# q of eight heads at a time by 64-row TensorE tiles, with VectorE's order set by deadlines, in an attention, mixer and MLP kernel

## The chip, the cores and the metric

One Trainium2 chip, one core. The metric is the device time of one execution in microseconds (us); lower is better. A kernel is run several times. With one core, a run counts as slow when it lies over 1.5% above the fastest of its kernel. A ratio is the mean time of one kernel's fast runs over the mean of the other's fast runs of the same rounds (for the experiments without the profiled run), so it isn't quite the ratio of the medians that are quoted beside it.

## The reference

```python
xn = layernorm(x)                                  # x [1, 2048, 576]
q  = xn @ wq                                       # 32 heads of 128; wq [576, 4096]
p  = softmax(q @ k.T * 128**-0.5)                  # k, v: the last 512 positions of the cache, 16 kv heads
s  = (p @ v).reshape(1, 2048, 4096) @ wo           # wo [4096, 576]
h  = gelu(layernorm(xn) @ w1)                      # mixer, w1 [576, 576]
hs = concat(the four quarters of h, shifted by 1, -1, 2, -2 rows) @ w2
x1 = xn + hs
g  = silu(x1 + gelu(layernorm(x1) @ w3) @ w4)      # MLP, w3 [576, 4608], w4 [4608, 576]
out = x + s * g
```

D is 576 = 4.5 x 128, so a contraction over D by 128-row matmuls has a last chunk that is half zeros. And the 2048 rows are done in four query blocks of 512; a block has 32 heads, called heads 0 to 31, 32 to 63 and so on.

## The kernel before

The parts that the change and the argument touch (cuts are marked `# ...`). q is made one head ahead, by five 128-row matmuls; scores of four key chunks, exps on ScalarE, values of two row tiles at a time, their evacuation on VectorE, and a DMA transpose of the head's output on SyncE's queue:

```python
def stage_q(u):
    # ...
    for kc in range(NDC):                                       # NDC = 5
        nc.tensor.matmul(psq[:, :], lhsT=w[:, kc, ...], rhs=xT_b[qb % 2][:, kc, :], ...)
    # copy to qT: VectorE in the first block, ScalarE in the others
def stage_s(u, kc):
    nc.tensor.matmul(sc[:, :], lhsT=kT[:, g, ...], rhs=qT_t[u][:, :], ...)
    nc.scalar.activation(out=pT[:, :], in_=sc[:, :], func=ACT.Exp, scale=SCALE)
def stage_v(u, t0):                                             # two row tiles of four matmuls each
    # ...
    with tc.high_priority(offset=HP):
        nc.vector.reciprocal(out=ri, in_=po[:, :, Dh])
        nc.vector.tensor_tensor(out=o[:, t0:t0 + 2, :], in0=po[:, :, 0:Dh], in1=ri..., op=ALU.mult)
def stage_t(u):
    nc.sync.dma_start(out=oT[:], in_=o[:]..., transpose=True)
```

In the first block, fetches of wq, wo, V, K and the mixer's w1 go on beside the heads, issued by GpSimd. A tiny copy of a head's first exp tile (`late`) holds GpSimd back until that head is reached:

```python
at(2, lambda: late(pT_t[2][0][0:1, 0:1], load_w1))
for i in range(8):
    at(4 + 3 * i, lambda i=i: late(pT_t[4 + 3 * i][0][0:1, 0:1], lambda: load_wo(i)))   # nc.gpsimd.dma_start
for j in range(2, NB * 8):
    at(4 * (j - 1) - 1, lambda j=j: load_wq(j))                                          # wq of 4 heads
```

Of the kernel before, what the change touches and what calls it, by code (L numbers as in the profile page):

```python
# [31 lines left out]
def kernel(  # L32
# [43 lines left out]
    PAD = 2  # L76
    VW = Dh + 2
    HP = 1500
# [20 lines left out]
    def rsqrt_newton(pool, var, n):  # L99
        v = pool.tile([P, n], FP32, name="nr_v")  # L100
        nc.vector.tensor_scalar(out=v[:], in0=var, scalar1=1.0, scalar2=LN_EPS, op0=ALU.mult, op1=ALU.add)
        y = pool.tile([P, n], FP32, name="nr_y")
        nc.vector.tensor_scalar(out=y[:].bitcast(I32), in0=v[:].bitcast(I32), scalar1=-0.5, scalar2=RSQRT_MAGIC,
                                op0=ALU.mult, op1=ALU.add)
        for _ in range(3):
            t = pool.tile([P, n], FP32, name="nr_t")
            nc.vector.scalar_tensor_tensor(out=t[:], in0=y[:], scalar=-0.5, in1=y[:], op0=ALU.mult, op1=ALU.mult)
            nc.vector.tensor_tensor(out=t[:], in0=t[:], in1=v[:], op=ALU.mult)
            y2 = pool.tile([P, n], FP32, name="nr_y")
            nc.vector.scalar_tensor_tensor(out=y2[:], in0=t[:], scalar=1.5, in1=y[:], op0=ALU.add, op1=ALU.mult)  # L110
            y = y2
        return y

    def rsqrt_table(pool, var, n):
        y = pool.tile([P, n], FP32, name="nr_y")
        nc.scalar.activation(out=y[:], in_=var, func=ACT.Sqrt, bias=eps_t[:])
        nc.vector.reciprocal(out=y[:], in_=y[:])
        e = pool.tile([P, 1], FP32, name="nr_e")
        nc.scalar.activation(out=e[:], in_=y[:, 0:1], func=ACT.Exp, scale=0.0)
        return y  # L120

    def layernorm_steps(pool, dsts, srcs, rsqrt=rsqrt_newton, twice=False):
        n = len(srcs)
        hw = D // 2
        st_ = {}

        def stats(i):
            if i == 0:
                st_["mv"] = pool.tile([P, n, 2], FP32, name="ln_mv")
            st = pool.tile([P, 2, 6], FP32, name="ln_st")  # L130
            for j in range(2):
                tc.keep_in_program_order(
                    nc.vector.bn_stats(out=st[:, j, :], in_=srcs[i][:, j * hw:(j + 1) * hw]))
            nc.vector.bn_aggr(out=st_["mv"][:, i, :], in_=st[:])

        def inv():
            st_["r"] = rsqrt(pool, st_["mv"][:, :, 1], n)

        def apply(i):
            parts = [(dsts[i], srcs[i])]  # L140
            if twice:
                parts = [(dsts[i][:, 0:D], srcs[i]), (dsts[i][:, D:DP], srcs[i][:, NF * P:D])]
            for dst, src in parts:
                nc.vector.tensor_scalar(out=dst, in0=src, scalar1=st_["mv"][:, i, 0:1],
                                        scalar2=st_["r"][:, i:i + 1], op0=ALU.subtract, op1=ALU.mult)

        return ([lambda i=i: stats(i) for i in range(n)] + [inv] + [lambda i=i: apply(i) for i in range(n)])

    def layernorm_small_steps(pool, dsts, srcs):

        n = len(srcs)
        hw = D // 2
        s = {}
        mv = pool.tile([P, n, 2], FP32, name="ln_mv")

        def stats(i, j):
            if j == 0:
                s["st"] = pool.tile([P, 2, 6], FP32, name="ln_st")
            nc.vector.bn_stats(out=s["st"][:, j, :], in_=srcs[i][:, j * hw:(j + 1) * hw])
            if j == 1:  # L160
                nc.vector.bn_aggr(out=mv[:, i, :], in_=s["st"][:])

        def begin():
            s["v"] = pool.tile([P, n], FP32, name="nr_v")
            nc.vector.tensor_scalar(out=s["v"][:], in0=mv[:, :, 1], scalar1=1.0, scalar2=LN_EPS, op0=ALU.mult,
                                    op1=ALU.add)
            s["y"] = pool.tile([P, n], FP32, name="nr_y")
            nc.vector.tensor_scalar(out=s["y"][:].bitcast(I32), in0=s["v"][:].bitcast(I32), scalar1=-0.5,
                                    scalar2=RSQRT_MAGIC, op0=ALU.mult, op1=ALU.add)

        def newton():
            y = s["y"]
            t = pool.tile([P, n], FP32, name="nr_t")
            nc.vector.scalar_tensor_tensor(out=t[:], in0=y[:], scalar=-0.5, in1=y[:], op0=ALU.mult, op1=ALU.mult)
            nc.vector.tensor_tensor(out=t[:], in0=t[:], in1=s["v"][:], op=ALU.mult)
            s["y"] = pool.tile([P, n], FP32, name="nr_y")
            nc.vector.scalar_tensor_tensor(out=s["y"][:], in0=t[:], scalar=1.5, in1=y[:], op0=ALU.add, op1=ALU.mult)

        def apply(i):
            for dst, src in [(dsts[i][:, D:DP], srcs[i][:, NF * P:D]), (dsts[i][:, 0:D], srcs[i])]:  # L180
                nc.vector.tensor_scalar(out=dst, in0=src, scalar1=mv[:, i, 0:1], scalar2=s["y"][:, i:i + 1],
                                        op0=ALU.subtract, op1=ALU.mult)

        return ([lambda i=i, j=j: stats(i, j) for i in range(n) for j in range(2)] + [begin, newton, newton, newton] +
                [lambda i=i: apply(i) for i in range(n)])

# [7 lines left out]
    xn_b = [keep.tile([P, TB, DP], BF16, name=f"xn_b{i}") for i in range(2)]  # L194
    xnn_b = keep.tile([P, TB, DP], BF16, name="xnn_b")
# [4 lines left out]
    xm_b = [xnn_b, xn_b[0]]  # L200
# [6 lines left out]
    def ln3_steps(b):  # L207
        xm = xm_b[b % 2]
        dsts, srcs = [xm[:, tt, :] for tt in range(TB)], [x1_t[b][:, tt, :] for tt in range(TB)]
        return layernorm_small_steps(small, dsts, srcs) if b else layernorm_steps(small, dsts, srcs, twice=True)  # L210

    def ln3_transpose(b):
        for tt in range(TB):
            nc.sync.dma_start(out=xT_b[b % 2][:, :, tt * P:(tt + 1) * P], in_=xm_b[b % 2][:, tt, :], transpose=True)

    with ExitStack() as actx:
# [17 lines left out]
        xraw = pool("xraw", 4)  # L234
        qT_pool = pool("qT_pool", 3)
        pT_pool = pool("pT_pool", 10)
        o_pool = pool("o_pool", 8)
        hb_pool = pool("hb_pool", 2)
        hs_pool = pool("hs_pool", 1)
        g1_pool = pool("g1_pool", 1)  # L240
# [11 lines left out]
        def load_x(b, eng):  # L252
            x_t[b] = []
            for tt in range(TB):
                xt = xraw.tile([P, D], BF16, name="xt")
                t = b * TB + tt
                eng.dma_start(out=xt[:], in_=x2[t * P:(t + 1) * P, :])
                x_t[b].append(xt)

        def load_wq(j, eng=None):  # L260
# [5 lines left out]
            eng.dma_start(out=w[0:DR, NF, :], in_=A_wq[NF * P:D, c0:c0 + 4 * Dh])  # L266
# [17 lines left out]
        def prep_k(g):  # L284
# [3 lines left out]
            def tr(kc):  # L288
# [4 lines left out]
                if kc == KCH - 1:  # L293
# [3 lines left out]
                    with tc.high_priority(offset=HP):  # L297
                        nc.vector.tensor_copy(out=kT[:, g, :], in_=st["ps"][:, :])
# [3 lines left out]
        def late(ap, fn):  # L302
            g = nc.gpsimd.tensor_copy(out=gate[:, :], in_=ap)
            with tc.issue_after(g.ins):
                fn()

        x_t[0] = []
        for tt in range(TB):
            xt = xraw.tile([P, D], BF16, name="xt")
# [809 lines left out]
```

## Time and profile before

| | |
|---|---|
| median of the first three runs | 846.1 us (843.39 to 848.49) |
| span of the profiled run | 842.4 us |
| TensorE, ScalarE, VectorE busy | 98, 55, 51% |
| attention and mixer, MLP and tail | 11.6 to 552.2, 552.2 to 842.4 us |

The prediction shows the lines that it rests on. One view it didn't take is the busy time by stage, with the first query block by itself: the first row is the first block (heads 0 to 31), the second the other three with the output projection, the third the MLP. A row gives the stretch and its length, the busy time of each engine with its instructions, the granted clock, the mean busy share of the DMA engines (the time that their packets took, over the time of 16 engines; it can exceed 1), and what they moved in GB/s.

```profile
11.60:115.30 103.70, 101.91 (x864) 63.93 (x881) 82.11 (x263) 77.59 (x138) 30.69 (x52) 1.00 0.90 185
115.30:552.20 436.90, 433.22 (x3603) 256.36 (x3663) 202.65 (x698) 278.70 (x512) 39.85 (x65) 1.00 0.47 102
552.20:842.40 290.20, 283.04 (x3348) 157.70 (x3349) 137.05 (x370) 100.63 (x170) 0.00 (x0) 1.00 0.22 60
```

TensorE is full in every stage. But the DMA engines are 90% busy in the first block, against 47 and 22% later. The page's own row of 40 slices says the same in its first five digits, if one looks at it: 6, 9, 9, 7, 8.

### The profile page before, as it was taken

How to read it: one execution, taken by the hardware profiler on the slowest of the kernel's cores; microseconds unless marked ns; L12 is line 12 of the kernel's file. 1: busy time of each engine (PE TensorE's matmuls, PEld its weight loads, DVE VectorE, ACT ScalarE, POOL GpSimd, SP SyncE). 2: the span in 40 equal slices, each digit the busy share in tenths (PEclk: the TensorE clock that was granted, in tenths of full speed). 3: DMA queues.
4: the chain of work that ended last, by engine and by line, in shares of the span. 5: the costliest groups of instructions: out<-in, count | busy, mean ns of one | idle time of the engine just before them, and what ended most of it. 6: DMA issues, size and time to landing. Idle time of an engine off the chain costs nothing.

```text
span 842.4 us, 19365 instructions
## 1 busy us (share of the span) xinstructions
PE 827.0 (98%) x7896; PEld 486.5 (58%) x7980; DVE 427.8 (51%) x1351; ACT 460.9 (55%) x825; POOL 76.5 (9%) x134
## 2 busy tenths in 40 slices
PE   8999999999999999999999999999999999999996
PEld 6665655665665566565566555455555555555555
DVE  5789941258751156772144884034246636555334
ACT  4776773498793388885369874033233333334610
POOL 3532213010010111010001100000000000000000
PEclk9999999999999999999999999999999999999999
DMA  6997862173372174363148336993001321230101
GB/s 173 228 248 163 147 137 65 56 137 90 87 135 46 41 131 97 89 121 79 29 87 160 67 85 106 282 340 83 2 2 44 64 69 44 46 87 16 44 15 46
DMA packets 139983, 83.94 MB, mean 100 GB/s; under 512 B 106944, under 2 KB 133248, under 8 KB 139888
## 3 DMA queue, kind: packets, MB, share of 16 engines
q1 hardware_dynamic: 130048, 53.01, 31.2%
q0 software_dynamic: 8448, 28.15, 11.9%
q8 instruction: 64, 1.05, 0.5%
q10 hardware_dynamic: 1392, 1.48, 0.5%
q14 instruction: 31, 0.25, 0.1%
HBM read 49.17 MB, written 9.44 MB: 70 GB/s over the span
## 4 chain that ended last, share of the span: by engine, by line

## 5 line engine op out<-in xcount | busy, mean ns | idle before, releaser
L404 ACT ACTIVATE pT<-sc 128x512 bf16<-128x512 f32 x512 | 290.3, 596 | 101.5 <-PE sc L402 89.5
L402 PE MATMUL sc<-qT,kT 128*128 128x512 bf16 x492 | 174.6, 378 | 1.3 <-DVE qT L392 0.6
L419 PEld LDWEIGHTS <-pT 128*128 128x128 bf16 x2048 | 139.6, 98 | 50.7 <-ACT pT L404 0.4
L419 PE MATMUL po<-v_sb,pT 128*128 128x129 bf16 x2048 | 161.4, 220 | 1.3 <-ACT pT L404 0.3
L387 PE MATMUL psq<-xT_b,wq_b 128*128 128x512 bf16 x604 | 152.4, 379 | 2.2 <-DVE xT_b L369 0.3
L423 DVE RECIPROCAL ri_b<-po 128x2 f32<-128x2 f32 x256 | 43.1, 168 | 188.8 <-PE po L419 184.5
L772 PE MATMUL ph<-xT_b,w_s 64*128 64x512 bf16 x976 | 127.1, 376 | 0.2 <-DVE hx L788 0.2
L809 PE MATMUL pm<-w_s,h 64*128 64x512 bf16 x864 | 122.3, 377 | 0.0
L443 PE MATMUL pswo<-wo_sb,oT 128*128 128x512 bf16 x497 | 114.2, 379 | 0.7
L424 DVE TENSOR_TENSOR o<-po,ri_b 128x256 bf16<-128x256 f32 x256 | 107.9, 422 | 6.5 <-DVE ri_b L423 0.3
L790 ACT ACTIVATE h<-ph 128x512 bf16<-128x512 f32 x67 | 39.4, 597 | 130.4 <-PE ph L772 130.4
L387 PEld LDWEIGHTS <-wq_b 128*128 128x128 bf16 x640 | 62.3, 98 | 74.3 <-issue 2.3
L809 PEld LDWEIGHTS <-h 64*128 64x128 bf16 x1728 | 70.7, 94 | 55.6 <-issue 0.4
L443 PEld LDWEIGHTS <-oT 128*128 128x128 bf16 x1024 | 65.0, 98 | 55.1 <-DMA oT<-o 0.2
L809 PE MATMUL pr<-w_s,h 64*128 64x64 bf16 x864 | 90.1, 189 | 0.2 <-ACT h L790 0.2
L772 PEld LDWEIGHTS <-w_s 64*128 64x128 bf16 x1152 | 57.2, 94 | 48.6 <-issue 0.5
L788 DVE COPY hx<-ph 128x512 f32<-128x512 f32 x55 | 38.0, 692 | 69.6 <-PE ph L772 69.6
L394 ACT ACTIVATE qT<-psq 128x512 bf16<-128x512 f32 x96 | 57.4, 598 | 27.8 <-PE psq L387 26.8
L402 PEld LDWEIGHTS <-kT 128*128 128x128 bf16 x512 | 47.4, 97 | 28.3 <-DVE qT L392 1.1
L264 POOL DMA_DIRECT2D wq_b<-in_A_wq_dram x30 | 23.3, 778 | 312.3 <-PE psq L387 293.5
L790 ACT ACTIVATE h<-hx 128x512 bf16<-128x512 f32 x55 | 34.6, 630 | 8.3 <-DVE hx L788 6.4
L762 DVE TENSOR_SCALAR fence<-ph,ph 1x1 f32<-1x1 f32 x61 | 12.8, 210 | 49.9 <-PE ph L772 49.4
(124 smaller groups left out, 645.4 us busy)
## 6 DMA issues: line engine op xcount, KB each, us to landing
wq_b<-in_A_wq_dram POOLq DMA_DIRECT2D x30, 512.0 KB, 5.2
w_s<-in_B_w_dram SPq DMA_DIRECT2D x9, 576.0 KB, 7.1
wo_sb<-in_A_wo_dram POOLq DMA_DIRECT2D x8, 576.0 KB, 5.0
w_s<-in_B_w_dram SPq DMA_DIRECT2D x9, 512.0 KB, 7.9
x_dram<-x SPq DMA_DIRECT2D x4, 576.0 KB, 3.5
x<-x_dram SPq DMA_DIRECT2D x4, 576.0 KB, 5.0
s_b<-s_dram SPq DMA_DIRECT2D x4, 576.0 KB, 5.6
x_b<-in_A_x_dram SPq DMA_DIRECT2D x4, 576.0 KB, 6.3
```

The lines of the kernel that those rows point to most:

```text
L387: nc.tensor.matmul(psq[:, :], lhsT=w[:, kc, hh * Dh:(hh + 1) * Dh], rhs=xT_b[qb % 2][:, kc, :], start=(kc == 0), stop=(kc == NDC - 1))
L394: nc.scalar.activation(out=qT[:, :], in_=psq[:, :], func=ACT.Copy)
L402: nc.tensor.matmul(sc[:, :], lhsT=kT[:, g, kc * P:(kc + 1) * P], rhs=qT_t[u][:, :], start=True, stop=True)
L404: nc.scalar.activation(out=pT[:, :], in_=sc[:, :], func=ACT.Exp, scale=SCALE)
L419: nc.tensor.matmul(po[:, j, :], lhsT=pTs[kc][:, tt * P:(tt + 1) * P], rhs=v_sb[:, g, kc, 0:Dh + 1], start=(kc == 0), stop=(kc == KCH - 1))
L423: nc.vector.reciprocal(out=ri, in_=po[:, :, Dh])
L424: nc.vector.tensor_tensor(out=o[:, t0:t0 + 2, :], in0=po[:, :, 0:Dh], in1=ri.unsqueeze(2).to_broadcast([P, 2, Dh]), op=ALU.mult)
L443: nc.tensor.matmul(ps, lhsT=oT_t[qb * Hq + h][:, tt, :], rhs=wo_sb[:, h, lo:hi], start=(h == 0), stop=(h == Hq - 1))
L772: nc.tensor.matmul(ps[i][:, :], lhsT=lhsT, rhs=xT[half, kc, :], start=first, stop=last, skip_group_check=True)
L788: nc.vector.tensor_copy(out=src[:, :], in_=ps[i][:, :])
L790: nc.scalar.activation(out=h3[:, :], in_=src[:, :], func=ACT.Gelu_apprx_tanh)
L809: nc.tensor.matmul(out, lhsT=h3_t[b, fc][half, tt * P:(tt + 1) * P], rhs=w4_s[fc // WS][half, fc % WS, lo:hi], start=key not in started, s ...
```

## The change

Its intent: two heads share the half chunk of D (64-row tiles that run in pairs), which takes 64 of 640 q slots off TensorE. To make that possible, q comes in groups of four heads in the first block and of eight later, gelu is written in place and buffers are shared so that eight q tiles fit, values come one row tile at a time and half a head later, and VectorE's and ScalarE's order is no longer loose but fixed, with layernorm and gelu steps let in by deadlines and a budget of time. The core of the diff, cut:

```diff
-            eng.dma_start(out=w[0:DR, NF, :], in_=A_wq[NF * P:D, c0:c0 + 4 * Dh])
+            for half in (LO, HI):
+                eng.dma_start(out=w[half, NF, :], in_=A_wq[NF * P:D, c0:c0 + 4 * Dh])
-        qT_pool = pool("qT_pool", 3)
+        qT_pool = pool("qT_pool", 8)
-        o_pool = pool("o_pool", 8)
+        o_pool = pool("o_pool", 9)
+        def stage_qs(u0, n):
+            # pairs of heads; banks X, Y, Z, X
+                    q_half(xT, u, ps, [(kc, ((0, LO), (1, HI))) for kc in range(NDC)], True)
+                    nc.vector.tensor_scalar(out=f[:, :], in0=ps[0][0:1, 0:1], scalar1=ps[1][0:1, 0:1], ...)  # fence
+                    unit(0.7)                       # up to 0.7 us of layernorm or gelu steps on VectorE
+                # ...
+                    q_half(xT, u, ps, [(kc, ((1, LO), (0, HI))) for kc in range(NF)], False)
+                    nc.scalar.activation(out=qT_t[u][:, :], in_=ps[0][:, :], func=ACT.Copy)
+                    nc.vector.tensor_copy(out=qT_t[u + 1][:, :], in_=ps[1][:, :])
-        at(2, lambda: late(pT_t[2][0][0:1, 0:1], load_w1))
-        at(10, gather_w1)
+        at(13, lambda: late(pT_t[13][0][0:1, 0:1], load_w1))
+        at(20, gather_w1)
-            at(4 + 3 * i, ... load_wo(i)))
+            at(9 + 3 * i, ... load_wo(i)))
-            at(4 * (j - 1) - 1, lambda j=j: load_wq(j))
+            at(4 * (j - 2) + 1 if j < 10 else 8 * (j // 2 - 1) + 1 + j % 2, lambda j=j: load_wq(j))
-        with tc.manual_schedule(engines={SP, POOL, PE}):
+        with tc.manual_schedule(engines={SP, POOL, PE, DVE, ACTE}):
+                if u % (4 if u < Hq else 8) == 0 and 0 < u < U:
+                    stage_qs(u, 4 if u < Hq else 8)
+                    v, tt = (u - 2, 2 + i) if i < 2 else (u - 1, i - 2)
```

## The prediction

> **What bounds the kernel now.** I read the page's busy table first, then TensorE's waits, then one head in the timeline, then the groups by line.
>
> ```profile
> PE 827.0 (98%) x7896; PEld 486.5 (58%) x7980; DVE 427.8 (51%) x1351; ACT 460.9 (55%) x825; POOL 76.5 (9%) x134
> ...
> PE warm L672 <- POOL ident masks.py:199: 1.6, 1, 1.6
> PE ps_k L291 <- DMA x<-in_A_k_cache_dram: 0.9, 1, 0.9
> PE sc L402 <- DVE qT L392: 0.6, 1, 0.6
> PE psq L387 <- DVE xT_b L369: 0.3, 1, 0.3
> PE sc L402 <- ACT pT L404: 0.3, 1, 0.3
> ```
>
> TensorE has work for 98% of the span, and its list of waits is short: the largest five (shown) sum to 3.7 us, nearly all in the first 16 us. So no wait can be shortened for profit, and time must come out of TensorE's own instruction slots. Busy time alone doesn't prove that the slots are dense, because a 512-column matmul is shown as 0.378 us and overlaps its successor. The timeline of one head in the second query block shows the spacing:
>
> ```profile
> 303.46 0.38 PE L402 MATMUL sc<-qT,kT 128*128 128x512 bf16 x1
> ...
> 303.67 0.63 PE L419 MATMUL po<-v_sb,pT 128*128 128x129 bf16 x8
> ...
> 304.14 0.38 PE L402 MATMUL sc<-qT,kT 128*128 128x512 bf16 x1
> ...
> 305.26 1.24 PE L387 MATMUL psq<-xT_b,wq_b 128*128 128x512 bf16 x5
> ...
> 306.34 0.38 PE L402 MATMUL sc<-qT,kT 128*128 128x512 bf16 x1
> ...
> 307.77 1.58 ACT L404 ACTIVATE pT<-sc 128x512 bf16<-128x512 f32 x3
> ```
>
> A head repeats every 306.34 - 303.46 = 2.88 us. Five q matmuls take 1.24, so one slot is (1.24 - 0.38)/4 = 0.215 us. Eight value matmuls fill 303.67 to 304.14, so one is 0.059. The head's slots are 5 x 0.216 for q + 4 x 0.216 for scores + 16 x 0.059 for values = 1.08 + 0.86 + 0.94 = 2.88 us: the measured period, with no gap. ScalarE's three exps in 1.58 us, one being 0.596 in the groups, give (1.58 - 0.596)/2 = 0.49 us apiece when they are queued.
>
> Summed over attention and mixer, with counts from the loops: q 640 x 0.216 = 138, scores 512 x 0.216 = 111, values 2048 x 0.059 = 120, output projection 512 x 0.216 + 512 x 0.029 = 125, mixer 180 x 0.216 + 80 x 0.029 = 41, K transposes 4, together 539 us. The first q is at 11.6 and the MLP starts at 552.3 (its row is below): 541 us. The MLP and its tail, to 842.4, are not changed.
>
> ```profile
> 551.32 1.01 PE L443 MATMUL pswr<-wo_sb,oT 128*128 128x64 bf16 x29
> 552.26 1.04 PE L772 MATMUL ph<-xT_b,w_s 64*128 64x512 bf16 x8
> 553.13 0.38 PE L772 MATMUL ph<-xT_b,w3r_s 64*128 64x512 bf16 x2
> ...
> 799.34 1.04 PE L772 MATMUL ph<-xT_b,w_s 64*128 64x512 bf16 x8
> 800.32 0.39 PE L972 MATMUL pm<-w_s,h 128*128 128x512 bf16 x1
> ```
>
> These rows are also the only two places where the kernel changes between 128-row and 64-row matmuls.
>
> **What the Trainium skill says.** "TensorE: Matmul & The Clock Gate", Part 3 on packing small matmuls, says that matmuls in distinct row groups run concurrently. The trace agrees: eight 64-row matmuls take 553.13 - 552.26 = 0.87 us, so a pair takes one slot of 0.217. "TensorEngine Tiling (Array Packing)", Key Properties, says that a change of tiling mode drains TensorE. The trace agrees and sizes it: the 29 narrow matmuls are (1.01 - 0.19)/28 = 0.029 apart, the last starts at 552.14, and the next, of 64 rows, only at 552.26, that is 0.12 against 0.03; on the way back four pairs from 799.34 should end at 800.20 and the next starts at 800.32. About 0.1 us each way. The same page, Gotcha 1, says that different row tiles must not access one PSUM bank at the same time; the kernel before already puts a tiny VectorE fence (210 ns) between the halves that swap banks in the MLP. Lastly, the first page says that ScalarE and VectorE are strict FIFO; so a wrongly placed VectorE instruction delays those behind it. No wait of the trace tests that as the order is now loose.
>
> **The change part by part.**
> (1) q by 64-row tiles. D is 576 = 4.5 chunks of 128 rows, and the fifth q matmul of each head is half zeros. Two heads now share the work: 9 half chunks x 2 heads = 18 half matmuls = 9 pair slots instead of 10. Over 128 heads: 64 slots x 0.216 = 13.8 us saved, all on the bound.
> (2) Mode switches. Eight groups of 4 heads in the first block and four groups of 8 in each of three others are 20 groups, 40 switches x 0.1 = +4.0 us. Some will hide in waits of (4).
> (3) Fences. 64 x 0.21 = 13 us more of VectorE. While one fence runs, TensorE does the other pair: the fence of the second pair must come within the first pair's second half, 4 slots = 0.86 us, against about 0.2 latency + 0.21 + at most 0.7 of an instruction ahead. It should be hidden.
> (4) ScalarE's pace. Before, q (1.08 us) stood between the scores of each head, giving ScalarE 2.88 us for four exps and a copy, 4 x 0.49 + 0.6 = 2.6. Now q comes in a lump of 36 slots = 7.8 us per 8 heads, in which ScalarE has only up to three leftover scores and four copies. Between lumps, a head without other TensorE work is 0.86 + 0.94 = 1.80 us for TensorE and 1.97 for ScalarE: 0.17 us of wait. Of the last three blocks' 96 heads about 60 have no filler by the new slots (the output projection sits in five heads of a block, the mixer in about ten). A group's start adds 0.3 (ScalarE's last q copy), and a run-ahead of three score banks takes away about 0.5. I count 1.3 + 1.9 + 1.3 us for these blocks. In the first block, q also takes two of the three score banks, hence waits for two exps: ScalarE's cycle per 4 heads is about 12.2 against 11.8 us, +0.4 in eight groups = 3.2. Sum of this part about +7.5 at most.
> (5) One bank for the output projection. Its evacuation (0.6 + 0.2 of latency) used to lie behind a q lump; now only a score and four values (0.45 us) stand in between, unless mixer atoms follow. Five such places x 0.4 = +2.
> (6) VectorE's order. VectorE gains 13 us of fences, 32 x 0.69 = 22 us of q copies (ScalarE loses as many) and 5 of zero padding: 428 to 468, 56% of the span. It isn't the bound, but a pair of value groups now comes every 0.9 us with a 0.6 us evacuation and two banks. A wide instruction in between can hold TensorE by 0.1 or 0.2. I give it +2.
> (7) In-place gelu, in-place layernorm, shared buffers: the same instructions; they pay with SBUF for eight q tiles. Nine instead of eight attention outputs give transposes slack: issuing one takes 1.2 us on the queue, a head at least 1.8, so no gain of its own.
> (8) Start: waits of 0.6 + 0.3 + 0.3 at the first heads go, -1; the last head's values come half a head later, +0.5.
> Parts (4) to (6) hold the same engine and overlap: while TensorE waits for a bank, ScalarE catches up. Of their 11.5 I keep 7. Sum: -13.8 + 4.0 + 7 - 0.5 = -3.3, that is 846.1 - 3.3 = 842.8; I say 842.
>
> **Rivals.** A: the waits are tuned away, the gain is slots less switches: 846.1 - 13.8 + 4.0 - 1 = 835. For it: the slots of the mixer are placed unevenly, as if by trial, and a deadline order looks made for this. Against: 0.17 us in each unfilled head isn't removable by order. B: ScalarE becomes the bound wherever there is no filler and the terms add fully, or the strict order on VectorE and ScalarE (a tanh queued ahead of exps while its input is late) stalls TensorE; 846.1 - 13.8 + 4 + 11.5 + 4 = 852. For it: ScalarE has 290 us of exps in some 510 us and is idle for about half of the lumps. Against: four copies fall into the lumps. C: the half matmuls don't pair (each needs its own weight load, 64 pairs more of them): then q costs more than before and the time rises by some 10 us. Against: the MLP's 64-row matmuls pair at 0.217.
>
> **Range and chances.** The floor is 835 less one or two, the upper rival 852. So 842, with 833 to 851 for 8 in 10. Faster by over 2% would be below 829, more than the whole saving of 13.8: 2%. Slower by over 2% is above 863, which takes stalls of 27 us: 4%. Within 2%: 94%.
>
> **What would show it.** q rows as 64-row matmuls, 18 per two heads at 0.108 us each; the first 64-row matmul of a lump about 0.1 late. TensorE's wait list, nearly empty now, should name the exps (score bank, and values waiting for exps) with 5 to 8 us in the heads without filler, and the output projection waiting for its own evacuation with about 2. The MLP should start near 548 instead of 552 and take the same 290 us. Wrong: if TensorE's waits on VectorE (fences, value evacuation) exceed those on ScalarE, part (6) was under-sized; if waits are under 3 us in all, rival A holds; if the MLP's length changes, I have missed something.

## The result, and the profile after

| | before | after |
|---|---|---|
| median | 844.91 us (4 runs) | 875.82 us (4 runs: 869.92, 871.14, 880.5, and 883.55, slow) |
| ratio of fast runs | | 1.0336, 95% interval 1.024 to 1.0432: slower |
| profiled run | 842.4 us span | 868.1 us span |
| first block | 103.7 us | 111.5 us |
| later blocks | 436.9 us | 454.6 us |
| MLP and tail | 290.2 us | 290.2 us |

The predicted 842 and its range up to 851 are missed. The same view by stage, for the changed kernel:

```profile
11.80:123.30 111.50, 100.14 (x967) 62.22 (x977) 71.87 (x242) 74.51 (x148) 35.23 (x60) 0.95 0.99 165
123.30:577.90 454.60, 440.62 (x4043) 258.69 (x4085) 258.80 (x824) 249.81 (x470) 50.29 (x86) 1.00 0.47 105
577.90:868.10 290.20, 282.63 (x3345) 161.88 (x3346) 137.71 (x374) 100.38 (x170) 1.09 (x1) 0.99 0.22 60
```

So the loss has two places: 7.8 us in the first block, where TensorE's busy time shrank while its clock fell to 0.95 and the DMA share rose to 0.99 with fewer GB/s (165 for 185), and 17.7 in the later blocks, where VectorE now has 258.8 us for 202.7. The MLP is untouched. TensorE's waits (us in total, times, longest), nearly empty before, name engines for both:

```profile
PE psq L444 <- DMA wq_b<-in_A_wq_dram: 7.3, 3, 5.2
PE po L469 <- DVE o L476: 6.5, 9, 1.4
PE psx L615 <- DVE x L626: 3.0, 5, 0.9
PE po L469 <- issue: 1.9, 12, 0.2
PE psq L444 <- DMA xT_b<-xn_b: 1.7, 1, 1.7
...
PE pswo L497 <- ACT x L511: 0.9, 4, 0.2
PE sc L452 <- ACT pT L454: 0.7, 1, 0.7
```

**The first block.** Its groups of four heads (from a group's first q matmul to the next group's) take 12.4, 12.1, 12.1, 12.1, 12.1, 14.4, 20.8 and 15.5 us: at first the pace that was predicted (12.2), and then a stall of some 12 us (11.5 against the first block of the run without a stall, h2_spq below). By stretches of the span, same columns as above:

```profile
20.00:55.00 35.00, 34.84 (x357) 22.64 (x358) 27.66 (x95) 25.87 (x53) 11.45 (x20) 1.00 0.77 154
55.00:75.00 20.00, 19.95 (x210) 13.18 (x210) 15.94 (x59) 15.20 (x31) 11.70 (x20) 1.00 1.10 205
75.00:95.00 20.00, 11.78 (x117) 7.07 (x116) 8.79 (x31) 9.14 (x18) 3.51 (x6) 0.85 1.06 113
```

In the third stretch the DMA engines are as busy as in the second and move little more than half as much, and TensorE works 11.78 of 20 us. The timeline shows the chain: SyncE's queue takes 37 us to issue six output transposes (the kernel before took 1.2 to 2.4 each); VectorE waits 7.42 us for an output buffer to be read out; TensorE waits 5.25 us for weights of the next q group.

```profile
59.69 37.33 SPq L486 DMA_TRANSPOSE oT<-o  x6
...
93.22 0.42 DVE L476 TENSOR_TENSOR o<-po,ri_b 128x256 bf16<-128x256 f32 x1 [7.42 <-DMA oT<-o]
...
94.46 5.57 PE L444 MATMUL psq<-xT_b,wq_b 64*128 64x512 bf16 x27 [5.25 <-DMA wq_b<-in_A_wq_dram]
```

The page's table of DMA issues gives KB and the median from issue to landing; the kernel before had 5.0 in the first of these two rows and 3.1 in the second:

```profile
wo_sb<-in_A_wo_dram POOLq DMA_DIRECT2D x8, 576.0 KB, 10.6
...
oT<-o SPq DMA_TRANSPOSE x128, 2.7
```

The row of `oT<-o` is a trap. Its median over the whole span even fell; but of the 32 transposes issued between 20 and 115 us, 13 landed after more than 9 us and the latest after 29.8. Before, none of 38 was above 9.0.

Not all of the 11.5 us is waiting. The granted clock was 0.50 from 89.1 to 99.3 us, so when the weights had come at 94.5 TensorE worked at this half clock for 4.8 us more, which I estimate from these figures at 2.4 us lost:

```profile
90.00:95.00 5.00, 0.54 (x4) 0.27 (x6) 0.75 (x2) 0.00 (x0) 0.00 (x0) 0.50 0.78 133
95.00:100.00 5.00, 5.00 (x28) 1.66 (x25) 1.26 (x4) 0.60 (x1) 0.00 (x0) 0.57 1.20 186
```

Other traces have such stretches, of 3.4 us or more, in the later blocks too. They are named below where they bear on a comparison.

**The later blocks.** The list of waits sums to some 12 us there, less than the loss. The rest is gaps too short for it: a 512-column matmul is drawn as 0.378 us, so a successor that is 0.27 us late isn't seen as late. The timeline of heads without filling work shows ScalarE with twelve exps end to end, and the scores at its pace:

```profile
363.35 6.04 ACT L454 ACTIVATE pT<-sc 128x512 bf16<-128x512 f32 x12
...
365.03 0.38 PE L452 MATMUL sc<-qT,kT 128*128 128x512 bf16 x1
...
366.01 0.38 PE L452 MATMUL sc<-qT,kT 128*128 128x512 bf16 x1
...
366.99 0.38 PE L452 MATMUL sc<-qT,kT 128*128 128x512 bf16 x1
```

Two scores per 0.98 us, where the slots of two scores and two groups of four values are 0.90. And where the mixer's second product has one bank, TensorE waits for VectorE to add it to xn and free the bank:

```profile
506.55 0.68 DVE L626 TENSOR_TENSOR x<-psx,xn_b 128x512 bf16<-128x512 f32 x1
507.28 1.02 PE L615 MATMUL psx<-w_sb,hb 128*128 128x512 bf16 x4 [0.93 <-DVE x L626]
```

I therefore took, for every matmul, the time to the next one's start less its slot, and added it up by the kinds of the two. In the later blocks (of the one-queue run below, which has them as the changed kernel does): scores followed by values 6.1 us (the bank that VectorE must free), values followed by scores 5.5 (ScalarE), values followed by the mixer's product 5.1, values followed by the output projection 3.1 (its one bank), going into 64-row mode 0.85 over nine and out about 1.3 over twelve, other kinds about 1. That is some 23. The same count gives 3.9 us in the kernel before.

### The profile page after: what moved, and what is told of

Its sections match the earlier page's. It is cut to its first block, busy times and chain, and to the rows that moved or that the text cites.

```text
span 868.1 us, 20505 instructions
## 1 busy us (share of the span) xinstructions
PE 831.8 (96%) x8436; PEld 490.2 (56%) x8492; DVE 475.4 (55%) x1463; ACT 428.6 (49%) x793; POOL 91.3 (11%) x161
## 4 chain that ended last, share of the span: by engine, by line
## 5 line engine op out<-in xcount | busy, mean ns | idle before, releaser
L454 ACT ACTIVATE pT<-sc 128x512 bf16<-128x512 f32 x512 | 266.8, 668 | 91.4 <-PE sc L452 89.8
L469 PE MATMUL po<-v_sb,pT 128*128 128x129 bf16 x2048 | 202.5, 220 | 9.0 <-DVE o L476 6.5
L469 PEld LDWEIGHTS <-pT 128*128 128x128 bf16 x2048 | 157.3, 97 | 82.4 <-DVE o L476 11.2
L452 PE MATMUL sc<-qT,kT 128*128 128x512 bf16 x489 | 184.6, 378 | 1.3 <-ACT pT L454 0.7
L444 PE MATMUL psq<-xT_b,wq_b 64*128 64x512 bf16 x1152 | 132.9, 381 | 9.9 <-DMA wq_b<-in_A_wq_dram 7.3
L476 DVE TENSOR_TENSOR o<-po,ri_b 128x256 bf16<-128x256 f32 x256 | 108.6, 424 | 17.7 <-DMA oT<-o 8.7
L868 PEld LDWEIGHTS <-h 64*128 64x128 bf16 x1728 | 73.5, 94 | 52.9 <-issue 0.3
L444 PEld LDWEIGHTS <-wq_b 64*128 64x128 bf16 x1152 | 58.7, 95 | 77.1 <-issue 8.4
L436 ACT ACTIVATE qT<-psq 128x512 bf16<-128x512 f32 x64 | 38.2, 597 | 96.7 <-PE psq L444 94.2
L452 PEld LDWEIGHTS <-kT 128*128 128x128 bf16 x512 | 49.9, 98 | 21.3 <-issue 8.8
L437 DVE CAST qT<-psq 128x512 bf16<-128x512 f32 x64 | 44.1, 690 | 18.4 <-PE psq L444 18.2
```

The source lines that it names most:

```text
L436: nc.scalar.activation(out=qT_t[u][:, :], in_=ps[0][:, :], func=ACT.Copy)
L437: nc.vector.tensor_copy(out=qT_t[u + 1][:, :], in_=ps[1][:, :])
L444: nc.tensor.matmul(ps[k][:, :], lhsT=w[half, kc, hh * Dh:(hh + 1) * Dh], rhs=xT[half, kc, :], start=(first and kc == 0), stop=(not first a ...
L452: nc.tensor.matmul(sc[:, :], lhsT=kT[:, g, kc * P:(kc + 1) * P], rhs=qT_t[u][:, :], start=True, stop=True)
L469: nc.tensor.matmul(po[:, j, :], lhsT=pTs[kc][:, tt * P:(tt + 1) * P], rhs=v_sb[:, g, kc, 0:Dh + 1], start=(kc == 0), stop=(kc == KCH - 1))
L868: nc.tensor.matmul(out, lhsT=h3_t[b, fc][half, tt * P:(tt + 1) * P], rhs=w4_s[fc // WS][half, fc % WS, lo:hi], start=key not in started, s ...
```

## The experiments

Two numbers from the packets of a trace serve in all of them, for 20 to 115 or 125 us: how late output and layernorm transposes land, and for how long both kinds of packets are in flight at a time (in steps of 0.25 us; more than two of each), with what each kind moved meanwhile. The table holds them, in the order of this section.

| run | us, median | transposes: latest landing, number over 9 us | both in flight, us | fetched + transposed then, KB per us |
|---|---|---|---|---|
| before | 844.91 | 9.0, 0 of 38 | 15.5 | 102 + 79 |
| after | 875.82 | 29.8, 13 of 32 | 38.5 | 117 + 42 |
| e1_loads | 889.87 | 27.6, 17 of 24 | 55.5 | 119 + 31 |
| b_late | 853.83 (fast runs 844.6, profiled, and 848.33) | 10.8, 3 of 38 | 17.2 | 126 + 72 |
| e2_q128 | 886.78 | 28.6, 14 of 25 | 65.0 | 117 + 29 |
| e3_b2banks | 885.22 | 26.5, 17 of 23 | 40.2 | 110 + 44 |
| f2_wo_first | 873.03, and 892.91, slow (profiled) | 26.2, 19 of 20 | 74.0 | 91 + 28 |
| f3_o4 | 877.72 and 880.44 | 25.2, 7 of 32 | 34.2 | 101 + 42 |
| g1_paced | 869.42 | 27.0, 10 of 31 | 42.0 | 123 + 42 |
| g2_block0 | 874.07 | 28.0, 15 of 30 | 56.2 | 114 + 40 |
| g4_relief2 | 871.65 | 12.9, 4 of 38 (the profiled run, 860.89) | 30.8 | 92 + 55 |
| h1_quarter_wo | 859.48 | 23.6, 12 of 33 | 42.2 | 90 + 42 |
| h4_before_more | 852.29 | 12.7, 8 of 33 | 22.2 | 138 + 72 |
| h2_spq | 857.46 | 7.4, 0 of 38 | 14.0 | 119 + 105 |
| i1_actq | 877.06 | 7.7, 0 of 33 | 15.2 | 106 + 86 |

With one kind alone in flight, the kernel before moves 289 KB per us of fetches, or 142 of transposes.

### Is the stall a matter of when the fetches come?

My first theory was that the later places of wo and w1 crowd the fetches. The first run puts them back, the second gives the kernel before the later places.

```diff
 e1_loads (from the changed kernel)
-        at(13, ... load_w1))
+        at(2, ... load_w1))
-            at(9 + 3 * i, ... load_wo(i)))
+            at(4 + 3 * i, ... load_wo(i)))
 b_late (from the kernel before)
-        at(2, ... load_w1))
+        at(10, ... load_w1))
-            at(4 + 3 * i, ... load_wo(i)))
+            at(9 + 3 * i, ... load_wo(i)))
```

> The changed kernel with one edit: the output projection's weights and w1 are fetched five and eleven heads earlier in the first block, as in the kernel before. Theory 1 (crowded loads): in the changed kernel about 15 us of the 25 us lost before the MLP come from 72 to 123 us, where oT transposes took up to 30 us to land, value evacuations waited 9 us for them and q 7 us for wq; the cause is that the fetches start late and pile up. Then this kernel lies near 855 us, transposes land within about 10 us and TensorE no longer waits for wq. Rival (the two half-row fetches of wq's last chunk, or the denser transposes, overload the queues whatever the timing): 868 to 876 and the same long landings.

> The mirror of it: the kernel before, with the output projection's weights fetched five heads later and w1 eight heads later. Theory 1: landing times of its transposes rise well over 10 us around 55 to 95 us and it loses some 5 to 15 us against 844. Rival (timing of the fetches doesn't matter): within 1 us of 844.

Measured: e1_loads 889.87 us, ratio 1.0533, so worse; the stall came earlier, with 22.9 us of VectorE's waits for output buffers and 21.9 us of TensorE's on VectorE's evacuation (16.2 of them in the first block). b_late 853.83, its profiled run 844.6 without a stall; two of its runs, 859.33 and 859.73, count as slow, and the ratio, 1.0106 (1.0021 to 1.0191), has them in it. Its fast runs, 844.6 and 848.33, lie among the kernel before's of the same rounds (843.39 to 850.76), so no loss is shown. The theory falls: the old places don't cure the changed kernel, and the new ones aren't shown to harm the old kernel.

### Is it the 64-row q, the half-row fetch, or VectorE?

Both from e1_loads: q by 128-row matmuls in the same groups, without fence and without the second fetch of the half chunk; and a second bank for the mixer's second product.

```diff
 e2_q128
-                    q_half(xT, u, ps, [(kc, ((0, LO), (1, HI))) ...      # and the fence, and the second half
+                    q_full(xT, u, ps)          # for k in 0, 1: five matmuls lhsT=w[:, kc, ...], rhs=xT[:, kc, :]
 e3_b2banks
-                    st["ps"] = ps_wo.tile([P, M0], FP32, name="psx1", tag="wo")
+                    psp, tag = (ps_pq, "pq") if tt % 2 else (ps_wo, "wo")
+                    st["ps"] = psp.tile([P, M0], FP32, name="psx1", tag=tag)
```

> The first experiment, with q again by five 128-row matmuls per head, in the same groups of 8 heads, without fences and without the second half-row fetch. Theory (as predicted: 64 slots of 0.216 saved, 40 mode switches of 0.1 paid): slower than the first experiment by 13.8 - 4.0 = about 10 us. Rival (64-row matmuls with fences bring less, or their waits eat it): slower by under 4 us.

> The first experiment, with the mixer's second product alternating between two accumulator banks instead of one. Theory 2: its TensorE waits for VectorE's evacuation, about 4.5 us in the changed kernel, go, and the kernel is 3 to 4 us faster than the first experiment. Rival (VectorE's strict order holds TensorE anyway and the wait moves to the value evacuation): within 1.5 us of it.

Measured: e2_q128 886.78 us, three of four runs slow, the profiled one too; but the eleven group periods of the later blocks can be compared where the granted clock is alike. At full clock they take 402.6 us in e2_q128 and 397.4 in the changed kernel, whose later blocks are those of e1_loads. e1_loads has 399.0 and e3_b2banks (885.22 us) 395.3, each with 3.4 us at half clock in its last group. So 64-row tiles save 5.2 us there, switches included, where the prediction's terms (1) and (2) give 7.3 for eleven groups; and a second bank for the mixer gives 3.7. Both still stall in the first block, so the stall needs neither the half-row fetch nor that one bank.

### A spoiled run, and two on fetches and buffers

f1_block0 gave q of the first block per head again, but I left the wq fetches where groups of four need them.

```diff
 f1_block0
+        def stage_q(u): ...            # five 128-row matmuls per head, in the first block
 f2_wo_first
-            at(9 + 3 * i, ... load_wo(i)))
+            at(i // 4, ... load_wo(i)))
 f3_o4
-        o_pool = pool("o_pool", 9)
+        o_pool = pool("o_pool", 4)
```

> The changed kernel with its first block of 32 heads as before: q per head, one head ahead, by five 128-row matmuls; blocks two to four keep groups of 8 heads by 64-row tiles. Fetching earlier made the jam worse (first experiment), so theory 1 fell. Theory 1b (lumps of q make the heads between them follow each other every 2.0 instead of 2.9 us, so transposes and fetches of the first block, near the limit of the DMA engines already, arrive in bursts and the queue never drains): the jam is gone, landings below 12 us, the first block takes about 104 us instead of 111 to 127, and the time is 852 to 858. Rival (the jam comes from something else of the change: in-place layernorm, shared buffers, nine output buffers, the two half fetches, the looser fetch order): the jam stays and the time is 868 or more.

> The changed kernel with all eight fetches of the output projection's weights in the first two heads (16 to 30 us), when the DMA engines are nearly idle. Theory 1b: 4.7 MB less of fetches in the crowded stretch; the jam is gone or much shorter, 853 to 862. Rival (it isn't the amount of fetches, but deep queues of transposes beside any fetch): about as before, 868 or more.

> The changed kernel with four instead of nine buffers for attention outputs, so that no more than four transposes can wait in the queue. Theory 1b (DMA is over-subscribed, buffers only hide it): TensorE waits earlier and longer, 870 to 890. Rival (many queued transposes themselves cause the slow landings): landings stay under 12 us and the time falls below 865.

f1_block0 took 929.25 us, and its waits say why:

```profile
PE psq L444 <- DMA wq_b<-in_A_wq_dram: 60.6, 8, 16.2
```

A fetch was placed ahead of its buffer's last reader in program order, so heads waited for, and used, the next group's weights; that it passed the comparison shows only that the comparison is coarse there. It tells nothing on the stall; g2_block0 below is the mended form. f2_wo_first (873.03, and 892.91, slow) keeps the stall with all of wo fetched in the first two heads. f3_o4 (877.72 and 880.44) keeps it with four output buffers, so a deep queue of transposes isn't what starts it.

### Does another order of the last layernorm help?

From the changed kernel, with two banks for the mixer, and the MLP's first layernorm moved behind the last head:

```diff
-        at(3 * Hq + 18, lambda: push(U - 3, ln_chain(lambda: ln3_steps(0), ...)))
+        at(U, lambda: push(U, ln_chain(lambda: ln3_steps(0), ...)))
```

> The changed kernel with the mixer's second product in two banks (worth 3.7 us in blocks two to four of an earlier pair of traces) and the MLP's first layernorm moved from the last heads to the final output projection, where VectorE idles. Theory 2 (VectorE's fixed order puts filler ahead of the value evacuation, where the heads leave it only 0.25 us in 0.9): from the start of the fifth-last block boundary, that is from the first q of the second block to the MLP, 454.6 us falls by 7 to 8 to about 447. Rival (the waits come back elsewhere): it falls by less than 4.5. The total stays noisy because of the first block.

880.04 us, ratio 1.0416. From the second block's first q to the MLP it took 458.5 us, where about 447 was expected. The last group's period fell from 32.0 to 27.5 us (31.8 with the two banks alone, in e3_b2banks), as VectorE had less between the values; but from there to the MLP it took 64.8 us for 57.3, with 6.8 us at half clock and a new wait, because the layernorm's transposes now stood on SyncE's queue ahead of the MLP's weights:

```profile
PE ph L832 <- DMA w_s<-in_B_w_dram: 4.3, 1, 4.3
```

The wait moved and was not removed.

### Bursts, the grouping of q, and relief for VectorE

The second theory on the stall: some 3 MB asked for within 8 us start a backlog. g1_paced spreads the fetches, about one per head; g2_block0 is the mended f1_block0, with q per head and the kernel before's places for every fetch of the first block; the other two add relief for VectorE in the later blocks to each.

```diff
 g1_paced
-            at(9 + 3 * i, ... load_wo(i)))                 # w1 from head 13 to 11; V from heads 0, 4, ... 20
+            uw = [2, 6, 10, 14, 16, 19, 22, 26][i]         # to heads 0, 3, 8, 15, 18, 23, each gated
 g2_block0
+            stage_q(u + 1)                                 # per head in the first block
+            at(4 * (j - 1) - 1 if j < 10 else ..., load_wq(j))    # w1 at 2, wo at 4 + 3 i, as before the change
 g3_relief = g1_paced, g4_relief2 = g2_block0, each with
-                    unit(0.7)
+                    unit(1.2)
-                    nc.vector.tensor_copy(out=qT_t[u + 1][:, :], in_=ps[1][:, :])
+                    nc.scalar.activation(out=qT_t[u + 1][:, :], ...)    # but for a group's last pair
+                    # and the two banks of e3_b2banks
```

> The changed kernel with nothing but its fetches in the first block spread out, about one per head (w1 at head 11, the eight parts of wo at heads 2, 6, 10, 14, 16, 19, 22 and 26, the V heads each where no other fetch is), so that no eight microseconds ask for more than about 2 MB. Theory 'burst' (the first block's stall is a backlog that starts when about 3 MB are asked for in a row): the stall is gone or down to a few microseconds, output transposes land within 12 us all through the first block, the first 32 heads take about 112 us and the kernel 853 to 860 us. Rival (the first block's demand as a whole, with groups of four heads that run at an even pace, is more than the queues deliver, however it is spread): a stall of 10 us or more stays and the kernel takes 868 us or more.

> A corrected form of the first-block run that was spoiled: the changed kernel with q of the first 32 heads made per head by five 128-row matmuls, as before the change, and with the kernel before's heads for every fetch of that block (wq, wo, w1); later blocks as in the changed kernel. If the stall belongs to q by groups of four together with the fetches it pulls forward: the first block runs as in the kernel before (about 104 us from head 0 to head 31, no wait for wq over 1 us) and the kernel takes 852 to 860 us, of which the later blocks' loss of about 18 us against the kernel before is the remainder. Rival (the nine output buffers, the in-place x, the order of VectorE or another part stalls the first block by itself): 868 us or more with waits for output buffers still there.

> The paced kernel with three reliefs for VectorE in the later blocks: the mixer's second product takes its banks in turn from two pools, all but the last two copies of a group's q are made by ScalarE, and filler steps of a group come in lumps of at most 1.2 us rather than 0.7. Theory (VectorE's queue in the later blocks, not TensorE's slots, costs some 11 us there: about 7 before the value matmuls and 4.5 before the mixer's bank): from the first q of the second block to the MLP's first matmul it takes 446 to 449 us in place of 454.6. Rival (ScalarE, whose exponentials are the pace there, takes over what VectorE gives up): 452 us or more, with the wait of the scores' banks longer by what the other waits lose.

> The corrected first-block form with the same three reliefs: if both losses are what I take them for, they add up: first block as in the kernel before, later blocks 6 to 8 us shorter than in the changed kernel, 844 to 852 us in all. Rival (they are one loss in two places): no faster than the better of the two runs it is made of.

Measured: g1_paced 869.42 us (864.62 to 873.37), ratio 1.0284: the stall stays, transposes land as late as 27 us. The burst theory falls. g2_block0 874.07, ratio 1.0398: so the grouping of q with its earlier fetches isn't the cause either. g3_relief 879.97, ratio 1.0405, and g4_relief2 871.65 (its profiled run 860.89, with a small stall), ratio 1.0332. From the second block's first q to the MLP it took 455.0, 456.2, 455.1 and 455.4 us in the four runs: the reliefs together gave nothing. The second bank's gain was given back in the second block's last group, 31.9 us for 28.3, where the waits for value banks rose from 1.5 to 3.1 us in g3_relief and, in both relief runs, 3.4 us were at half clock; which of the other two edits raised the waits wasn't tried by itself.

### Bytes, or the way they are fetched?

What was left is in the last column of the table above. When both kinds are in flight, all stalled runs move only 28 to 44 KB per us of transposes; the kernel before moves 79. A head's transposes are 131 KB, with the layernorms' (eight of 164 KB per block) 172 KB. At 42 KB per us that is 172 / 42 = 4.1 us per head against a pace of 12.1 / 4 = 3.0, so a backlog, once there, grows while fetches last; at 79 it is 2.2 us, and a backlog drains. Three runs: less to fetch in the changed kernel, more to fetch in the kernel before, and the same bytes from SyncE's queue. h1_quarter_wo gives a wrong result (three quarters of wo are not fetched).

```diff
 h1_quarter_wo
-        for i in range(8):                              # rhs=wo_sb[:, h, lo:hi]
+        for i in (0, 1):                                # rhs=wo_sb[:, h % 8, lo:hi]
 h2_spq (every fetch of the first block but x)
-            nc.gpsimd.dma_start(out=wo_sb[:, h0:h0 + 4, :], ...
+            nc.sync.dma_start(out=wo_sb[:, h0:h0 + 4, :], ...
-            ... load_wq(j))
+            ... load_wq(j, nc.sync if j < 10 else None))    # V, K and w1 likewise, and no gate before them
 h4_before_more (from the kernel before)
             at(4 + 3 * i, ... load_wo(i)))
+            at(5 + 3 * i, ... load_wo(i)))
```

> The changed kernel with only two of wo's eight parts fetched in the first block (heads 9 and 12) and the attention output's projection reading those two for all heads: a wrong result on purpose, the same instructions on every compute engine, 3.5 MB less to fetch. Theory 'saturation' (with fetches alone the trace moves 288 KB per us and with transposes alone 142, but with both in flight only 157 to 180 together; the first block asks for 19 MB in 97 us, more than the mixed rate, so a backlog once started never drains): with 15.5 MB in 97 us the backlog drains, the stall is gone or under 4 us, output transposes land within 12 us, and the kernel takes 853 to 861 us. Rival (the stall comes from the order of the work, nine output buffers or VectorE, not from the sum of bytes): stall of 10 us or more, 868 us or more.

> The changed kernel with all fetches of the first block issued from SyncE, in one queue with the transposes, in place of GpSimd's own queue. If it is the mixing of fetch and transpose packets that loses the throughput, one queue takes them mostly in turn: less time with both in flight than the 38 us of the changed kernel (20 us or less), stall under 5 us, 853 to 862 us. Rival (the engines take packets of a queue no more in order than of two, or the sum of bytes alone is too much): both in flight as before or more, 868 us or more; a transpose behind a fetch in the queue may then even land later.

> The kernel before, with every part of wo fetched twice in the first block, the second time one head after the first: 4.7 MB more to fetch, nothing else. Saturation: the kernel before has 81 per cent of its first block's time taken by transfers at the rates that they reach alone, this makes it 97 per cent; its first block then stalls as the changed kernel's does, transposes land after 15 us or more, and it takes 855 to 875 us. Rival (the stall belongs to the changed kernel's order): within 1 per cent of the kernel before.

Measured: h1_quarter_wo 859.48 us, ratio 1.0176. TensorE's stall is nearly gone (2.5 us of waits on VectorE's evacuation in the first block), as expected; but 12 of 33 transposes still land after more than 9 us. So fewer bytes make the backlog bearable and don't remove it. h4_before_more 852.29 (851.64 to 862.33), ratio 1.0134: slower than the kernel before, by less than the 11 us and more that were expected. Its first block takes 112.4 us for 103.7. Its transposes land after up to 12.7 us, and it waits once for wq:

```profile
PE psq L387 <- DMA wq_b<-in_A_wq_dram: 6.4, 1, 6.4
```

h2_spq settles most: 857.46 us (856.21 to 859.04), ratio 1.0155 (1.012 to 1.019), with all of the changed kernel's bytes and its compute order. By stage (first and later blocks), and by two stretches of the first block:

```profile
11.70:111.70 100.00, 98.53 (x967) 62.48 (x977) 70.48 (x238) 73.98 (x148) 2.44 (x5) 0.99 0.96 191
111.70:566.10 454.40, 440.60 (x4042) 258.78 (x4081) 260.19 (x829) 250.22 (x471) 50.11 (x86) 1.00 0.45 103
```
```profile
55.00:75.00 20.00, 19.95 (x212) 13.46 (x212) 16.11 (x60) 16.33 (x33) 0.00 (x0) 1.00 1.10 238
75.00:95.00 20.00, 19.89 (x206) 12.86 (x205) 14.37 (x49) 14.54 (x30) 0.00 (x0) 1.00 1.13 185
```

The first block takes 100.0 us for 111.5, with the DMA engines just as busy as in the stall and 185 GB/s for 113. So it isn't the number of bytes by itself, though bytes count too (h1_quarter_wo, h4_before_more); the same bytes go through when they are issued from SyncE. The later blocks are the same to 0.2 us, which makes their 17.7 us a loss of its own.

### One queue, or smaller packets? And what is left

Issued from SyncE, the fetches also go out in packets of 1.0 and 1.2 KB, where GpSimd's were 4.1 and 4.6 KB. i1_actq issues them from ScalarE: small packets, but another queue than the transposes'. i2_spq_banks and i3_all add to h2_spq the mixer's two banks, and then two banks for the projection and a better spread of the mixer.

```diff
 i1_actq: as h2_spq, with nc.scalar in place of nc.sync
 i2_spq_banks = h2_spq with the two banks of e3_b2banks
 i3_all = i2_spq_banks with
-                    st[tt] = psp.tile([P, M0], FP32, name="pswo", tag=tag)
+                    p2, t2 = (psp, tag) if tt % 2 == 0 else (ps_pq, "pq")
+                    st[tt] = p2.tile([P, M0], FP32, name="pswo", tag=t2)
-            o2 = 22 if b == 1 else 10
+            o2 = 22 if b == 1 else 18 if b == 2 else 10          # and two products of a block 10 heads apart, not 6
```

> The changed kernel with the first block's fetches issued from ScalarE's queue, so that they go out as the same small packets as in the one-queue run (1.0 and 1.2 KB in place of 4.1 and 4.6) but still in another queue than the transposes. If the one queue is what cured the stall: transposes land after 15 us or more again and TensorE waits for output buffers, 865 us or more. If the small packets cured it: landings under 10 us, no such waits; ScalarE then loses its time for some 30 issues in the first block, so 857 to 866 us. TensorE's waits and the landings decide, not the total.

> The one-queue run with the mixer's second product taking its banks in turn from two pools. The same edit took 3.7 us off eleven group periods of a stalling kernel; if the losses of the later blocks are independent of the first block's, it takes 3 to 5 us off here: 852.5 to 854.5 us. Rival (the wait moves to another bank): 856 us or more.

> The same with the output projection's banks in turn from two pools too, and the mixer's second products of the third and fourth block moved to heads that have no filling work. If each of the waits found is its own: the projection's bank gives about 2 us, the moved products 1 to 2 us, 849 to 852 us; still slower than the kernel before. Rival (VectorE's queue is the one cause and takes the time back elsewhere): no better than 853 us.

i1_actq took 877.06 us, in its total like the stalled kernels, but for another reason. No transpose lands after more than 7.7 us, both kinds are in flight for 15.2 us, and no wait for output buffers or weights is in the first block; what TensorE waits for there is ScalarE, which loses its time to the issues:

```profile
PE sc L452 <- ACT pT L454: 14.4, 12, 5.5
```

So one queue isn't needed for the cure. One doubt stays: i1_actq's first block lasted 118.1 us, so it asked for less per us; but h1_quarter_wo, with 3.5 MB of some 19 less to fetch, kept 12 late landings. (Neither run has the gate that holds fetches back; but their timing alone was moved in four runs above without a cure.)

So in the changed kernel the transposes are held up beside fetches that GpSimd issues, in large packets, and not beside the same fetches from SyncE or ScalarE. Such fetches aren't enough by themselves: the kernel before has the same packets from GpSimd, and moves 79 KB per us of transposes beside them. A later count of the DMAs under way (issued, not landed), while both kinds of packets are in flight, shows where the two differ. With 2 or 3 plain DMAs under way the kernel before moves 72 and 83 KB per us of transposes; the changed kernel moves 95 with 3 (for 4.5 us), and 26 and 24 with 7 and 8 (for 22 us). h2_spq and i1_actq never had more than 5. Whether that depth is the cause of the slow transposes or only their mark isn't shown.

The Trainium skill says in "DMA: Bandwidth & Descriptors", Queues, rings and completion order, that each DMA engine goes round-robin between its queues, a whole packet at a turn. If the packets of the trace are such turns, turns of 4.6 KB in place of 1.2 would slow the transposes' 256-byte packets (a 4.6 KB packet took 0.25 us in the kernel before, a 1.2 KB one 0.07 in h2_spq). But no run shows the turns, and none separates the size of the packets from GpSimd's way of building them or from the depth, so which of them it is stays open.

i2_spq_banks took 853.66 us (853.0 to 856.47), 3.8 less than h2_spq's median, which is of other rounds, as expected. i3_all took 854.22: the gaps before the projection's matmuls fell from 3.1 to 1.1 us and the eleven group periods from 395.1 (with 3.4 us at half clock) to 391.3, and the total stayed, as its rival said. The last group took the gain back: from its first q to the MLP 61.9 us for 57.3, with 3.4 us at half clock and this wait:

```profile
501.72 0.16 DVE L104 TENSOR_SCALAR nr_v<-ln_mv 128x4 f32<-128x4 f32 x1
...
503.69 0.16 DVE L115 SCALAR_TENSOR_TENSOR nr_y<-nr_t,nr_y 128x4 f32<-128x4 f32 x1
...
504.31 0.41 DVE L642 TENSOR_TENSOR x<-psx1r,xn_b 128x256 bf16<-128x256 f32 x1
504.77 9.61 PE L444 MATMUL psq<-xT_b,wq_b 64*128 64x512 bf16 x71 [2.55 <-DVE x L642]
```

TensorE's q waits for a bank that VectorE's add of the mixer (L642) frees. The add's last matmul starts at 501.71, but eleven small steps of a layernorm and a value evacuation stand before it in the fixed order. Two edits were made at once, so what the projection's second bank gives alone isn't shown. Neither run beats the kernel before (844.4 in these rounds). Some runs of that kernel, 849.5 to 852.9 us at a clock of 0.994, may have had a short stall of their own; no trace of one is kept.

## Why the prediction was wrong

It said 842 us (833 to 851), 94% within 2%; it was 875.8, slower. By its own steps:

- **(1), (2) 64-row tiles and switches: right in kind, too large.** Pairs run as predicted. A switch cost 0.09 us in and 0.11 out, for the predicted 0.1. But the net gain of the two in eleven groups was 5.2 us, not 7.3 (e2_q128 against the changed kernel). I take the rest to be slots taken off TensorE where VectorE or ScalarE sets the pace; no run shows it.
- **(3) fences: hidden** in the changed kernel; four other runs have one wait each for a fence (f4_ln3 3.9 us, g3_relief 2.4, f3_o4 1.5, h1_quarter_wo 1.0).
- **(4) ScalarE's pace: right.** First-block groups took 12.1 us without a stall (12.2 predicted), and the gaps of values followed by scores were 5.5 us in the later blocks (4.5 predicted).
- **(5) one bank for the projection: right in size as a gap** (a second bank took 2.0 us off the gaps). What it gives as time isn't shown: i3_all, which changed the mixer's places too, stayed at i2_spq_banks' total.
- **(6) VectorE's order, "I give it +2": mis-sized.** The gaps it makes before values (6.1 us) and before the mixer's product (5.1) are about 11 (TensorE's list of waits names VectorE for 5.7 and 2.8 of them). The working looked at VectorE's share of the span (56%); in the later blocks its busy time rose by 56 us, and the wide steps come in the same heads as the two-bank evacuations. The prediction itself named this sign of an under-sized part (6): TensorE's waits on VectorE exceed those on ScalarE. A second mixer bank gave 3.7 and 3.8 of it back. Rival B's second half, that strict order stalls TensorE, came nearest, and was given 852. i3_all shows such a wait; but no run loosened the order alone, so how much of the 11 is order and how much VectorE's added load stays open.
- **(7) "Nine instead of eight attention outputs give transposes slack: issuing one takes 1.2 us on the queue, a head at least 1.8, so no gain of its own": the step that failed.** It took the issue time of a transpose in an uncrowded queue as a constant. In the stall six took 37 us. The sum has no term for transfers at all, although the first block had its DMA engines 90% busy. In the profiled runs the stall is 111.5 - 100.0 = 11.5 us; by medians of different rounds, 875.8 against h2_spq's 857.5, it is 18.
- **The keep of 7 of 11.5** was too hopeful. The later blocks should have gone from 436.9 less 3.9 of gaps to 424.7: less 10.4 for 48 slots, plus 2.1 for work that moved in from the first block (three pieces of the mixer at 1.08 less about 1.1 of values). They took 454.6, so gaps are 30 us; the count by kinds names 23. The remaining 7 I can't place; records that the trace lacks hide some.

So the two failures share the miss: without the stall, the changed kernel is at 857, outside the range too, 5 us above rival B and 14 above the kernel before.

What stays open besides the packets: why few fetches are under way at a time in the kernel before and not in g2_block0, which has its fetch places and its q. The changed kernel fetches less until 55 us (154 GB/s; the kernel before 231 in the same stretch), so more is left for later; but that wasn't tried by itself.

## What to carry to other kernels

Before counting slots, read busy time by stage for every engine, DMA too: a stage whose transfers are near full can't be sped up without asking for more per microsecond, and there a median landing over the whole span hides a backlog. If busy DMA engines move little, look at which packets are in flight together; moving the plain fetches from GpSimd's queue to SyncE's took 18 us off here by medians (11.6 between the profiled runs), with no byte less; ScalarE's queue cured the landings too, but cost ScalarE 25.8 us for 48 issues. When the engines' order is fixed by hand, size each engine's load within the heads where the fixed order is tight, not over the span, and count gaps from start to start. Before comparing stretches of two traces, look at the granted clock in each.

## What the Trainium skill lacked or had wrong

- "TensorEngine Tiling (Array Packing)", Key Properties, says that a mode switch drains TensorE, without a size: 0.09 us into 64-row mode and 0.11 out of it in these traces.
- "DMA: Bandwidth & Descriptors", Rules for kernel authors, says that spreading DMAs over SyncE, ScalarE and GpSimd doesn't help bandwidth. No run here tests spreading as such, and the page does advise SyncE for plain loads. What it doesn't size is the choice of engine beside DMA transposes: in the same stretch of the first block 113 GB/s with fetches from GpSimd, 185 with the same bytes from SyncE.
- The same page, Queues, rings and completion order, has the round-robin by packets but not what it does to DMA transposes beside large fetches: in the changed kernel they landed after up to 29.8 us beside packets of 4.1 to 4.6 KB from GpSimd (9.0 in the kernel before, where fewer were under way), after 7.4 to 7.7 at the most beside packets of 1.0 to 1.2 KB from SyncE or ScalarE.
